# Decode attention on one core: five of eight block copies moved from VectorE to GpSimd, and 96 identity transposes between pairs on TensorE

## The chip, the core and the metric

The kernel runs on one core of a Trainium2 chip. The core has a matrix engine (TensorE, PE in the profile, with its weight loads as PEld), VectorE (DVE), ScalarE (ACT), GpSimd (POOL) and SyncE (SP), and 16 DMA engines that move data between HBM and the on-chip memory SBUF. Each engine works through its own queue in order; engines wait for each other by semaphores. TensorE writes to PSUM, and other engines take the results from there. The metric is the device time of one execution in microseconds (us).

## The reference

Attention for a single query position, with 32 query heads that share 8 key and value heads in groups of four, 65,536 keys and a head width of 128, all in bf16.

```python
B, Hq, Hkv, Sq, Sk, D = 1, 32, 8, 1, 65536, 128
k = jnp.repeat(k, rep, axis=1)          # rep = 4
v = jnp.repeat(v, rep, axis=1)
scores = jnp.einsum("bhqd,bhkd->bhqk", q, k) * D ** -0.5
p = jax.nn.softmax(scores, axis=-1)
return jnp.einsum("bhqk,bhkd->bhqd", p, v)
```

K and V have 134 MB each, and every byte is read once.

## The kernel before

**Tiles and stages.** The keys of one head are split into four units of 16,384 keys; a unit is 128 partitions by T = 128 columns of keys, 4 MB of K and 4 MB of V. Two units make a pair, and NP = 16 pairs are worked through one after the other: two pairs for each of the eight heads. In each pair the even unit is n = 0 and the odd unit n = 1.

**Buffers.** `kbuf` has room for two units of K, `vbuf` for two of V, and `bbuf` for one more unit of K. In the pairs 1 to 12 (`WHOLE = (1, 13)`) one DMA loads both units of K into `kbuf`, and engines then copy the odd unit into `bbuf` in eight blocks of 128 x 2048 elements (`CB = 16` columns each), so that `kbuf` is free for the next pair while the odd unit is still being worked on. In the pairs 0, 13, 14 and 15 the odd unit's K is loaded straight into `bbuf`, and no copies run.

**Order of loads.** SyncE issues all loads in a written-out order: K of a pair, then V of it, then K of the next. The K load of pair p waits for `kfree` (the even unit of the pair before is transposed) and for 2p counts of `cfree` (its copies are done; two engines count one each per pair). The V load waits for `vfree` (the pair before has used its V). Loads run one behind the other in the DMA queue, so that a load that is issued before the one ahead of it has landed follows it without a hole.

**Work of a pair on TensorE** (`pe_pair`). For each of 16 groups of eight columns a unit's K is transposed into PSUM (`pe_transposes`, L131; four buffers `trb`), and three groups later (`LAG = 3`) the scores are computed from the evicted transposes `ktb` (`pe_scores`, L140). The odd unit's groups follow the even unit's in the same stream. Then come the products with V of both units (`pe_values`, L157, with the rescaled sum of the unit before added at L150). Before the first group of a load TensorE waits for that load, and in the odd unit before each block of 16 columns for the copy of that block (`cpd` if VectorE made it, `cpa` if ScalarE).

**Evictions and copies.** VectorE evicts three of four groups from PSUM to `ktb` (L196), ScalarE each fourth (L193). Between evictions of the even unit VectorE copies the blocks 0, 1, 2 (after group 2) and 3, 4 (after group 8) at L203, and ScalarE the blocks 5, 6 and 7 (after groups 3, 7 and 11) at L342. `copy_unit` holds the condition on the lap: outside the pairs 1 to 12 it only counts the semaphores.

**Softmax.** VectorE reduces a unit's scores to a maximum for each partition (`chunk_max`, L228), GpSimd takes the maximum over partitions (L373), VectorE forms the new running maximum (`new_max`, L238 to L240), ScalarE the exponentials (L333). In VectorE's queue the `new_max` of the even unit stands between the odd unit's evictions 4 and 5. At the end of a head GpSimd adds the sums over partitions (L375). GpSimd has no other work in the loop.

**Loops.** TensorE's loop has a turn for each pair, those of VectorE, ScalarE and GpSimd one for each head, so two pairs.

Of the kernel before, what the change touches and what calls it, by code (L numbers as in the profile page):

```python
# [10 lines left out]
P = 128  # L11
T = 128
TB = 8
# [2 lines left out]
NKG = 8  # L16
LAG = 3
CB = 16
HU = 4
Q = 32  # L20

# [4 lines left out]


WHOLE = (1, 13)
DVE_COPIES = {2: (0, 1, 2), 8: (3, 4)}
ACT_COPIES = {3: (5,), 7: (6,), 11: (7,)}  # L30

OUT_ROWS = ((16, 12), (15, 13), (14, 9, 5), (11, 10, 6, 1))
# [2 lines left out]
def on_act(j):  # L35
    return j % 4 == 3


def starts(sizes):
    return [sum(sizes[:i]) for i in range(len(sizes))]  # L40


def take(e, sem, n=1):

    e.wait_ge(sem, n)
    e.sem_inc(sem, -n)  # L46


def bass_standalone__gqa_softmax__decode_kernel(nc, q, k, v, out):
    _, Hq, _, D = q.shape  # L50
    _, H, Sk, _ = k.shape
    R = Hq // H
    HR = H * R
    NU = H * HU
    NP = NU // 2
    assert HR == Q and all(sum(x) == HR - R for x in OUT_ROWS) and D == P and Sk == P * T * HU and T * R == 512 and H >= 3 and HU == 4
    scale = float(D) ** -0.5
# [5 lines left out]
    def sb(name, shape, dt):  # L63
        return S(nc.sbuf_tensor(name, shape, dt))

    def sem(name):
        return S(nc.semaphore(name))
# [10 lines left out]
    ident = sb("ident", [P, P], DT.bfloat16)  # L78
# [21 lines left out]
    trb = [S(nc.psum_tensor(f"trb{i}", [P, TB * P], DT.bfloat16)) for i in range(NTB)]  # L100
# [4 lines left out]
    kp = [[sem(f"kp{i}_{p}") for p in range(len(K_PIECES[i]))] for i in range(2)]  # L105
    vp = [[sem(f"vp{i}_{p}") for p in range(len(V_PIECES[i]))] for i in range(2)]
    kfree, cfree, bfree = sem("kfree"), sem("cfree"), sem("bfree")
    cpd, cpa = sem("cpd"), sem("cpa")
    vfree = sem("vfree")
    trd, tra, evd, eva = sem("trd"), sem("tra"), sem("evd"), sem("eva")  # L110
    qkd, qrdy, pvd = sem("qkd"), sem("qrdy"), sem("pvd")
# [2 lines left out]
    xd, xa, xg = sem("xd"), sem("xa"), sem("xg")  # L114
# [3 lines left out]
    def own(e, ins, s):  # L118
        ins.then_inc(s, 1)
        take(e, s)  # L120


    def pe_transposes(pe, n, j):
        kv = (bbuf if n else kbuf)[:, 0:T * D].rearrange("p (t d) -> p t d", d=D)
        if j * TB in starts(K_PIECES[n]):
            take(pe, kp[n][starts(K_PIECES[n]).index(j * TB)], 16)
        if n and j * TB % CB == 0:
            take(pe, cpa if j * TB // CB in sum(ACT_COPIES.values(), ()) else cpd)
        for i in range(TB):
            t = j * TB + i  # L130
            ins = pe.transpose(trb[j % NTB][:, i * P:(i + 1) * P], kv[:, t, :], ident[:, :])  # L131
        ins.then_inc(tra if on_act(j) else trd, 1)

    def pe_scores(pe, n, j):
        take(pe, eva if on_act(j) else evd)
        if n == 0 and j == 0:
            take(pe, qrdy)
        for i in range(TB):
            t, off = j * TB + i, (j % NKG * TB + i) * P
            ins = pe.matmul(qkb[n][:, t * R:(t + 1) * R], lhsT=ktb[:, off:off + P],  # L140
                            rhs=qcur[:, :], start=True, stop=True)
        if j == G - 1:
            ins.then_inc(qkd, 1)

    def pe_values(pe, n):
        vv = vbuf[:, n * T * D:(n + 1) * T * D].rearrange("p (t d) -> p t d", d=D)
        for t in range(T):
            if t == T - V_PIECES[1][-1]:
                take(pe, acr)
                pe.matmul(pvb[n][:, 0:R], lhsT=identf[:, :], rhs=acc[:, :], start=False, stop=False)  # L150
            if t == 0:
                take(pe, vp[n][0], 16)
                take(pe, exd)
            piece = vp[n][starts(V_PIECES[n]).index(t)] if t and t in starts(V_PIECES[n]) else None
            if piece:
                pe.wait_ge(piece, 16)
            ins = pe.matmul(pvb[n][:, 0:R], lhsT=vv[:, t, :], rhs=pts[n][:, t * R:(t + 1) * R],  # L157
                            start=t == 0, stop=t == T - 1)
            if piece:
                pe.sem_inc(piece, -16)  # L160
        ins.then_inc(pvd, 1)

    def pe_pair(pe):
        pend = []
        for n in range(2):
            for j in range(G):
                pe_transposes(pe, n, j)
                pend.append((n, j))
                if len(pend) > LAG:
                    pe_scores(pe, *pend.pop(0))  # L170
        while pend:
            pe_scores(pe, *pend.pop(0))
        for n in range(2):
            pe_values(pe, n)

    def tensor_engine(pe):
        pe.wait_ge(q_sem, 16)
        pe.wait_ge(t_id, 1)
        pe.transpose(qps[:, 0:HR], qsb[:, :], ident[0:HR, 0:HR]).then_inc(s_x, 1)
        pe.wait_ge(t_if, 1)  # L180
        with pe.Fori(0, NP):
            pe_pair(pe)
        pe.wait_ge(t_f, H)
        pe.transpose(trb[0][0:R, 0:P], oT[:, HR - R:HR], ident[:, :]).then_inc(s_x, 1)  # L184

# [12 lines left out]
    def copy_unit(e, lap, second, copies, op, done, x):  # L198

        def copies_now():  # L200
            for c in copies:
                off = T * D + c * CB * D
                ins = op(bbuf[:, c * CB * D:(c + 1) * CB * D], kbuf[:, off:off + CB * D])  # L203
                if c != copies[-1]:
                    ins.then_inc(done, 1)
            own(e, ins, x)
            e.sem_inc(done, 1)

        lo, hi = ((w - second + 1) // 2 for w in WHOLE)
        with e.If(lap < hi):  # L210
            if lo:
                with e.If(lap >= lo):
                    copies_now()
                with e.Else():
                    e.sem_inc(done, len(copies))
            else:
                copies_now()
        with e.Else():
            e.sem_inc(done, len(copies))
# [7 lines left out]
    def chunk_max(e, n):  # L227
        e.tensor_reduce(cmax[:, :], qkb[n][:, :].rearrange("p (t g) -> p g t", g=R),  # L228
                        AX.X, ALU.max).then_inc(cm, 1)
# [19 lines left out]
            own(e, e.tensor_tensor(lp[:, :], lp[:, :], alpha[:, :], ALU.mult), xd)  # L249
            own(e, e.tensor_tensor(lp[:, :], lp[:, :], rsum[:, :], ALU.add), xd)  # L250

    def dve_pair(e, second, lap):

        fresh, last = not second, second
        if fresh:
            e.memset(acc[:, :], 0.0).then_inc(acr, 1)
        for j in range(G):
            if not on_act(j):
                evict(e, 0, j)
            if j in DVE_COPIES:  # L260
                copy_unit(e, lap, second, DVE_COPIES[j], e.tensor_copy, cpd, xd)
                if j == max(DVE_COPIES):
                    e.sem_inc(cfree, 1)
        for j in (0, 1, 2):
            evict(e, 1, j)
        take(e, qkd)
        chunk_max(e, 0)
        evict(e, 1, 4)
        new_max(e, 0, fresh)
        for j in (5, 6, 8, 9, 10):  # L270
            evict(e, 1, j)
        rescale(e, 0, fresh)
        if fresh:
            own(e, e.tensor_copy(otmp[:, 0:HR - R], oT[:, R:HR]), xd)
            own(e, e.tensor_copy(oT[:, 0:HR - R], otmp[:, 0:HR - R]), xd)
            e.transpose(orow[:, :], oT[:, :]).then_inc(t_o, 1)
        for j in (12, 13, 14):
            evict(e, 1, j)
        take(e, qkd)
        chunk_max(e, 1)  # L280
        if last:
            next_queries(e)
        else:
            e.sem_inc(qrdy, 1)
        new_max(e, 1, False)
        take(e, pvd)
        rescale(e, 1, False)
        if last:
            e.sem_inc(lrd, 1)
            take(e, lra)  # L290
            own(e, e.reciprocal(recip[:, :], la[:, :]), xd)
        e.wait_ge(pvd, 1)
        if last:
            e.tensor_tensor(oT[:, HR - R:HR], pvb[1][:, 0:R], recip[:, :], ALU.mult).then_inc(t_f, 1)  # L294
        e.sem_inc(pvd, -1)
        e.sem_inc(vfree, 1)  # L296
# [16 lines left out]
    def vector_engine(e):  # L313
        make_identity(e)
        own(e, e.memset(oT[:, :], 0.0), xd)
        e.wait_ge(s_x, 1)
        own(e, e.tensor_copy(qT[:, :], qps[:, 0:HR]), xd)
        next_queries(e)
        with e.Fori(0, H) as lap:
            dve_pair(e, False, lap)  # L320
            dve_pair(e, True, lap)
        e.wait_ge(s_x, 2)
        e.tensor_copy(lrow[:, :], trb[0][0:R, 0:P]).then_inc(t_row, 1)  # L323

# [42 lines left out]
    def gpsimd_engine(e):  # L367
        own(e, e.memset(lw[:, :], 0.0), xg)
        own(e, e.partition_all_reduce(la[:, :], lw[:, :], P, bass.bass_isa.ReduceOp.add), xg)
        with e.Fori(0, H):  # L370
            for u in range(HU):
                take(e, cm)
                e.partition_all_reduce(cmaxa[:, :], cmax[:, :], P, bass.bass_isa.ReduceOp.max).then_inc(cma, 1)  # L373
            take(e, lrd)
            e.partition_all_reduce(la[:, :], lp[:, :], P, bass.bass_isa.ReduceOp.add).then_inc(lra, 1)  # L375
# [93 lines left out]
```

## Time and profile before

| | |
|---|---|
| median of 3 runs | 629.8 us (629.59 to 630.06) |
| the profiled execution, its own time | 631.18 us |
| its span, from the first to the last instruction | 629.8 us |
| HBM read | 268.44 MB, 426 GB/s over the span |
| busy: PE, PEld | 501.8 us (80%), 492.4 us (78%) |
| busy: DVE, ACT, POOL | 343.7 us (55%), 249.2 us (40%), 16.1 us (3%) |
| mean granted TensorE clock | 0.794 |

Busy time is that of the whole span. A row of a timeline gives the start, the duration, the engine, the line, the operation with output and input, the number of like instructions that it merges, and in brackets the idle time before it with what ended it. PEq, DVEq and so on are the sequencers of the engines, which handle waits and semaphores. A row of windows gives a stretch, its length, the busy time and instructions of PE, PEld, DVE, ACT and POOL, the granted TensorE clock (1.00 is full speed), the mean busy share of the DMA engines and what they moved in GB/s. The share is put together from whole packets and can come out over 1 in a short stretch. Ends of TensorE's matmuls are modelled, so rows of one stream overlap.

### The profile page before, as it was taken

Reading aid. Unit: us, or ns where it says so; the run is one execution under the profiler, and the core shown is the slowest. Engines: PE = TensorE matmul, PEld = TensorE weight load, DVE = VectorE, ACT = ScalarE, POOL = GpSimd, SP = SyncE. Lnnn points to the kernel's source line nnn. Section 1 sums busy time; section 2 is a strip of 40 time slices with the busy share of each in tenths; the row PEclk is TensorE's granted clock in tenths of the full one; section 3 lists DMA queues with packets and bytes.
Section 4 is the critical chain, followed back from the end, with each engine's and each line's share of the span. In section 5 each row is a group of like instructions: output and inputs, shape, how many; then the busy total and the mean of one; then the engine's idle time right before and its main releaser. Section 6 shows DMA issues by size and latency. Waiting matters only on the chain. (4 is left out here: it accounts for less than half of the span.)

```text
span 629.8 us, 28624 instructions
## 1 busy us (share of the span) xinstructions
PE 501.8 (80%) x12354; PEld 492.4 (78%) x12354; DVE 343.7 (55%) x735; ACT 249.2 (40%) x447; POOL 16.1 (3%) x46
## 2 busy tenths in 40 slices
PE   5753896969969599696996968879697799889896
PEld 5743886958968599686986968879697799889895
DVE  4530763818548185471845718467283665647381
ACT  2320642616436164361644517345172552514151
POOL 0000000000000000000000000000000000000000
PEclk9875885958869588795977959779597897869595
DMA  8999999999999999999999999999999999999997
GB/s 356 438 448 422 437 429 437 429 433 433 437 425 425 450 420 445 416 445 408 454 416 433 429 437 429 437 429 441 425 450 416 450 408 458 408 433 431 417 439 288
DMA packets 7635, 268.59 MB, mean 426 GB/s; under 512 B 1096, under 2 KB 1096, under 8 KB 1992
## 3 DMA queue, kind: packets, MB, share of 16 engines
q1 hardware_dynamic: 7576, 268.45, 99.2%
q8 instruction: 6, 0.10, 0.1%
q14 instruction: 5, 0.04, 0.0%
q10 hardware_dynamic: 48, 0.01, 0.0%
HBM read 268.44 MB, written 0.01 MB: 426 GB/s over the span
## 5 line engine op out<-in xcount | busy, mean ns | idle before, releaser
L196 DVE COPY ktb<-trb 128x1024 bf16<-128x1024 bf16 x384 | 249.7, 688 | 161.1 <-DVEq L46 156.8
L193 ACT ACTIVATE ktb<-trb 128x1024 bf16<-128x1024 bf16 x128 | 131.1, 1024 | 321.9 <-ACTq L46 321.9
L131 PE MATMUL trb<-ident,kbuf 128*128 128x128 bf16 x2048 | 177.1, 244 | 69.5 <-PEq L46 69.5
L131 PEld LDWEIGHTS trb<-ident,kbuf 128*128 128x128 bf16 x2048 | 143.9, 111 | 70.6 <-issue 70.6
L140 PE MATMUL qkb<-qcur,ktb 128*128 128x4 bf16 x4096 | 175.9, 165 | 25.0 <-PEq L46 24.2
L140 PEld LDWEIGHTS qkb<-qcur,ktb 128*128 128x128 bf16 x4096 | 155.9, 97 | 31.1 <-issue 30.2
L131 PE MATMUL trb<-ident,bbuf 128*128 128x128 bf16 x2048 | 156.8, 219 | 4.4 <-issue 4.4
L157 PEld LDWEIGHTS pvb<-pts,vbuf 128*128 128x128 bf16 x4096 | 119.3, 104 | 25.3 <-issue 24.1
L157 PE MATMUL pvb<-pts,vbuf 128*128 128x4 bf16 x4096 | 117.6, 166 | 23.6 <-PEq L46 13.3
L131 PEld LDWEIGHTS trb<-ident,bbuf 128*128 128x128 bf16 x2048 | 117.4, 97 | 4.6 <-issue 4.6
L342 ACT ACTIVATE bbuf<-kbuf 128x2048 bf16<-128x2048 bf16 x36 | 68.5, 1902 | 0.0
L333 ACT ACTIVATE pts<-qkb,negm 128x128 bf16<-128x128 f32 x128 | 50.8, 548 | 0.0
L203 DVE COPY bbuf<-kbuf 128x2048 bf16<-128x2048 bf16 x60 | 38.0, 684 | 0.0
L333 ACT ACTIVATION_READ_ACCUMULATOR pts<-qkb,negm 128x1 f32 x128 | 35.6, 278 | 0.0
L228 DVE TENSOR_REDUCE cmax<-qkb 128x4 f32<-128x512 f32 x32 | 21.9, 686 | 16.8 <-DVEq L46 16.8
L247 DVE TENSOR_TENSOR acc<-pvb,alpha 128x4 f32<-128x4 f32 x24 | 3.9, 162 | 46.0 <-DVEq L46 45.9
L373 POOL PARTITION_ALL_REDUCE cmaxa<-cmax x32 | 11.9, 371 | 567.9 <-POOLq L46 567.9
L329 ACT ACTIVATE alpha<-dm 128x4 f32<-128x4 f32 x24 | 4.9, 202 | 46.2 <-ACTq L46 46.2
L150 PE MATMUL pvb<-acc,identf 128*128 128x4 f32 x64 | 18.2, 354 | 0.0
L150 PEld LDWEIGHTS pvb<-acc,identf 128*128 128x128 f32 x64 | 16.1, 312 | 0.0
L294 DVE TENSOR_TENSOR oT<-pvb,recip 128x4 bf16<-128x4 f32 x8 | 1.3, 162 | 17.4 <-PE pvb L157 17.4
L238 DVE TENSOR_TENSOR m<-m,cmaxa 128x4 f32<-128x4 f32 x24 | 3.9, 163 | 8.0 <-DVEq L46 7.8
(38 smaller groups left out, 39.6 us busy)
## 6 DMA issues: line engine op xcount, KB each, us to landing
vbuf<-in_v_dram SPq DMA_DIRECT2D x5, 4096.0 KB, 30.2
bbuf<-in_k_dram SPq DMA_DIRECT2D x4, 2048.0 KB, 22.0
kbuf<-in_k_dram SPq DMA_DIRECT2D x2, 4096.0 KB, 19.3
bbuf<-in_k_dram SPq DMA_DIRECT2D x2, 4096.0 KB, 18.6
kbuf<-in_k_dram SPq DMA_DIRECT2D x2, 2048.0 KB, 18.9
kbuf<-in_k_dram SPq DMA_DIRECT2D x4, 512.0 KB, 12.1
kbuf<-in_k_dram SPq DMA_DIRECT2D x2, 1024.0 KB, 14.5
vbuf<-in_v_dram SPq DMA_DIRECT2D x1, 2048.0 KB, 30.2
```

The source lines that it names most:

```text
L131: ins = pe.transpose(trb[j % NTB][:, i * P:(i + 1) * P], kv[:, t, :], ident[:, :])
L140: ins = pe.matmul(qkb[n][:, t * R:(t + 1) * R], lhsT=ktb[:, off:off + P], rhs=qcur[:, :], start=True, stop=True)
L150: pe.matmul(pvb[n][:, 0:R], lhsT=identf[:, :], rhs=acc[:, :], start=False, stop=False)
L157: ins = pe.matmul(pvb[n][:, 0:R], lhsT=vv[:, t, :], rhs=pts[n][:, t * R:(t + 1) * R], start=t == 0, stop=t == T - 1)
L193: e.activation(dst, trb[j % NTB][:, :], AF.Copy).then_inc(eva, 1)
L196: e.tensor_copy(dst, trb[j % NTB][:, :]).then_inc(evd, 1)
L203: ins = op(bbuf[:, c * CB * D:(c + 1) * CB * D], kbuf[:, off:off + CB * D])
L228: e.tensor_reduce(cmax[:, :], qkb[n][:, :].rearrange("p (t g) -> p g t", g=R), AX.X, ALU.max).then_inc(cm, 1)
L329: e.activation(alpha[:, :], dm[:, :], AF.Exp, scale=scale)
L333: ins = e.activation(pv[:, g, :], sv[:, g, :], AF.Exp, bias=negm[:, g:g + 1], scale=scale, accum_out=rsum[:, g:g + 1])
L342: return e.activation(o, i, AF.Copy)
L373: e.partition_all_reduce(cmaxa[:, :], cmax[:, :], P, bass.bass_isa.ReduceOp.max).then_inc(cma, 1)
```

## The change

GpSimd copies blocks 0 to 4 of the odd unit, in one go, after VectorE has queued the eviction of the pair's first group (`pgo`); VectorE copies none any more. The semaphore `cpd` becomes `cpg`, and GpSimd gives the second count of `cfree`. The max over partitions stands behind the copies in GpSimd's queue. After the products with V of a pair, in the laps 0 to 11, TensorE transposes the identity matrix into the PSUM buffer `trb0`, six turns of a loop with 16 transposes each; nobody reads the result. In the laps 12 to 15 the condition skips it.

```diff
+WARM = 6
-DVE_COPIES = {2: (0, 1, 2), 8: (3, 4)}
+POOL_COPIES = (0, 1, 2, 3, 4)
 ACT_COPIES = {3: (5,), 7: (6,), 11: (7,)}
...
-    cpd, cpa = sem("cpd"), sem("cpa")
+    cpg, cpa, pgo = sem("cpg"), sem("cpa"), sem("pgo")
...
         if n and j * TB % CB == 0:
-            take(pe, cpa if j * TB // CB in sum(ACT_COPIES.values(), ()) else cpd)
+            take(pe, cpa if j * TB // CB in sum(ACT_COPIES.values(), ()) else cpg)
...
-    def pe_pair(pe):
+    def pe_pair(pe, lap):
...
         for n in range(2):
             pe_values(pe, n)
+        with pe.If(lap < WHOLE[1] - 1):
+            with pe.Fori(0, WARM):
+                for i in range(16):
+                    pe.transpose(trb[0][:, 0:P], ident[:, :], ident[:, :])
...
-        with pe.Fori(0, NP):
-            pe_pair(pe)
+        with pe.Fori(0, NP) as lap:
+            pe_pair(pe, lap)
...
-    def dve_pair(e, second, lap):
+    def dve_pair(e, second):
...
             if not on_act(j):
                 evict(e, 0, j)
-            if j in DVE_COPIES:
-                copy_unit(e, lap, second, DVE_COPIES[j], e.tensor_copy, cpd, xd)
-                if j == max(DVE_COPIES):
-                    e.sem_inc(cfree, 1)
+            if j == 0:
+                e.sem_inc(pgo, 1)
...
-        with e.Fori(0, H):
+        with e.Fori(0, H) as lap:
             for u in range(HU):
+                if u % 2 == 0:
+                    take(e, pgo)
+                    copy_unit(e, lap, u // 2, POOL_COPIES, e.tensor_copy, cpg, xg)
+                    e.sem_inc(cfree, 1)
                 take(e, cm)
                 e.partition_all_reduce(cmaxa[:, :], cmax[:, :], P, bass.bass_isa.ReduceOp.max).then_inc(cma, 1)
```

More of the change, by code (lines that the diff above doesn't have):

```diff
@@ L318, in vector_engine @@
         next_queries(e)
-        with e.Fori(0, H) as lap:
-            dve_pair(e, False, lap)
-            dve_pair(e, True, lap)
+        with e.Fori(0, H):
+            dve_pair(e, False)
+            dve_pair(e, True)
         e.wait_ge(s_x, 2)
```

## The prediction

> **What bounds the kernel now.** I read the DMA busy share by stretches first, then SyncE's issues, then TensorE's timeline around one pair, then VectorE and ScalarE in the same stretch.
>
> ```profile
> 99.00:500.00 401.00, 320.88 (x7890) 315.08 (x7891) 227.31 (x472) 173.86 (x289) 9.58 (x25) 0.79 1.00 432
> 500.00:590.00 90.00, 81.81 (x2112) 80.87 (x2109) 52.62 (x113) 34.00 (x75) 2.66 (x7) 0.82 0.99 427
> 590.00:626.00 36.00, 31.49 (x782) 31.05 (x779) 19.49 (x42) 11.47 (x26) 1.17 (x3) 0.78 0.99 418
> ...
> 593.04 33.03 DMA vbuf<-in_v_dram
> ```
>
> The last three columns are TensorE's granted clock, the DMA share and GB/s. The 16 DMA engines are full (share 1.00, 432 GB/s) for 401 us, and the chain that ended last is one load of V until 626.07. The time is the transfer of 268 MB, provided that the next transfer is always issued before the running one ends. So I ask of every edit only whether it makes an issue late.
>
> ```profile
> 193.33 0.33 SPq L399 DMA_DIRECT2D kbuf<-in_k_dram  x1
> 213.71 0.33 SPq L420 DMA_DIRECT2D vbuf<-in_v_dram  x1
> 233.01 0.33 SPq L399 DMA_DIRECT2D kbuf<-in_k_dram  x1
> 253.55 0.33 SPq L420 DMA_DIRECT2D vbuf<-in_v_dram  x1
> ```
>
> ```profile
> 219.51 3.57 PE L131 MATMUL trb<-ident,kbuf 128*128 128x128 bf16 x32 [6.11 <-PEq L46]
> 222.88 0.40 PE L140 MATMUL qkb<-qcur,ktb 128*128 128x4 bf16 x8
> ...
> 232.71 0.61 PE L131 MATMUL trb<-ident,bbuf 128*128 128x128 bf16 x8
> ...
> 244.67 3.17 PE L157 MATMUL pvb<-pts,vbuf 128*128 128x4 bf16 x120
> ...
> 252.87 0.35 PE L157 MATMUL pvb<-pts,vbuf 128*128 128x4 bf16 x8
> 258.12 3.41 PE L131 MATMUL trb<-ident,kbuf 128*128 128x128 bf16 x32 [4.90 <-PEq L46]
> ...
> 271.33 0.61 PE L131 MATMUL trb<-ident,bbuf 128*128 128x128 bf16 x8
> ...
> 296.84 3.57 PE L131 MATMUL trb<-ident,kbuf 128*128 128x128 bf16 x32 [5.34 <-PEq L46]
> ```
>
> TensorE starts a pair when its K has landed: 219.51, 258.12, 296.84, a period of (296.84-219.51)/2 = 38.7 us. It works until 253.22 (33.7 us) and 291.50 (33.4 us), so P = 33.55 us, and stands still about 5.2 us. The V load of the next pair is issued at 253.55, when the products with V are done, 4.6 us before the running K load lands. The K load is issued at 233.01, 13.5 us after the start, while V needs half a period, 19.35 us. These two margins are what the change can use up; nothing it gains beyond them shortens the transfer.
>
> **The change: the transposes of the identity.** A block of 96 follows pairs 0 to 11. Its price hangs on the clock.
>
> ```profile
> 209.50:212.50 3.00, 3.00 (x116) 3.00 (x116) 0.47 (x3) 0.00 (x0) 0.00 (x0) 0.50 1.06 459
> ...
> 258.10:261.10 3.00, 2.98 (x29) 3.00 (x30) 1.49 (x3) 0.00 (x0) 0.00 (x0) 0.50 1.06 459
> 261.60:264.60 3.00, 2.52 (x61) 2.35 (x57) 2.46 (x5) 2.82 (x2) 0.00 (x0) 1.00 0.81 350
> 297.00:302.00 5.00, 5.00 (x61) 5.00 (x60) 3.68 (x6) 1.47 (x2) 0.00 (x0) 0.50 1.03 446
> ```
>
> ```profile
> 195.81 0.61 PE L131 MATMUL trb<-ident,bbuf 128*128 128x128 bf16 x8
> 196.25 0.34 PE L140 MATMUL qkb<-qcur,ktb 128*128 128x4 bf16 x8
> ```
>
> The four-column products with V leave the clock at 0.50 though TensorE is busy all the time. The next pair starts cold and is granted 1.00 after 3.0 us (start 258.12) to 5.2 us (start 296.84). A cold transpose takes 3.37/32 = 0.105 us (219.51 to the first scores at 222.88), a warm one 0.44/8 = 0.055 us. So 28 to 49 of the 96 run cold and the other 68 to 47 warm: 6.7 to 7.7 us, middle 7.2.
>
> The block sits in a loop of six turns under a condition, which no row shows on TensorE.
>
> ```profile
> 523.39 0.35 PE L157 MATMUL pvb<-pts,vbuf 128*128 128x4 bf16 x8
> 523.61 3.57 PE L131 MATMUL trb<-ident,kbuf 128*128 128x128 bf16 x32
> ...
> L256 DVE MEMSET acc<- 128x4 f32 x8 | 0.5, 62 | 4.1 <-issue 3.7 <-DVEq L46 0.3
> ```
>
> At one turn of the outer loop TensorE goes on 0.22 us after its last eight products with V began, as within a row: the turn cost nothing, because instructions were queued ahead. VectorE lost 3.7/7 = 0.53 us at each of its turns. Bounds 0 and 6 x 0.53 = 3.2 us; I take 0.3, nearest TensorE's own rows. The block is W = 7.5 us (6.7 to 10.9) where the gap was 5.2.
>
> After pair 0 the gap is longer, but there code may still be on its way:
>
> ```profile
> 46.80 1.52 PE L157 MATMUL pvb<-pts,vbuf 128*128 128x4 bf16 x51 [6.10 <-issue]
> ...
> 63.66 3.37 PE L131 MATMUL trb<-ident,kbuf 128*128 128x128 bf16 x32 [7.11 <-PEq L46]
> ```
>
> 7.5 against 7.11 makes pair 1 late by x0 = 0.4 us; one more stall like the 6.10 (waiting on nothing the profile shows, in the first lap alone) would make it 6.5. I take 0.4.
>
> **What the even unit gains.** VectorE loses its copies, and TensorE starts warm.
>
> ```profile
> 220.67 0.69 DVE L196 COPY ktb<-trb 128x1024 bf16<-128x1024 bf16 x1 [10.31 <-DVEq L46]
> ...
> 222.99 1.89 DVE L203 COPY bbuf<-kbuf 128x2048 bf16<-128x2048 bf16 x3
> 225.41 2.49 DVE L196 COPY ktb<-trb 128x1024 bf16<-128x1024 bf16 x4 [0.54 <-DVEq L46]
> 227.82 1.28 DVE L203 COPY bbuf<-kbuf 128x2048 bf16<-128x2048 bf16 x2
> ```
>
> ```profile
> 223.21 1.02 ACT L193 ACTIVATE ktb<-trb 128x1024 bf16<-128x1024 bf16 x1 [14.05 <-ACTq L46]
> ...
> 226.44 1.02 ACT L193 ACTIVATE ktb<-trb 128x1024 bf16<-128x1024 bf16 x1 [0.42 <-ACTq L46]
> ...
> 233.06 1.02 ACT L193 ACTIVATE ktb<-trb 128x1024 bf16<-128x1024 bf16 x1 [0.55 <-ACTq L46]
> ```
>
> The even unit takes 13.2 us (219.51 to 232.71) whether the clock rises early (258.12 to 271.33) or late: two engines that copy between evictions set it. VectorE loses 1.89 + 1.28 = 3.2 us of copies, and is no limit after that. ScalarE keeps a cycle of 3.23 us (223.21 to 226.44) for four blocks, against TensorE's 4 x 0.645 = 2.6 (0.44 + 0.20 a block). Warm, the first four transposed blocks take 1.8 us in place of 3.4, so ScalarE's first eviction starts 2.1 us into the pair (now 3.7) and its fourth at 2.1 + 3 x 3.23 = 11.8, done at 12.8. TensorE reaches the odd unit at 1.78 + 12 x 0.645 + 0.2 = 9.7, plus some 0.7 for ScalarE's third eviction: 10.4. There it waits about 0.6 for the fourth. The rest, 244.67 - 232.71 = 11.96 us, is in step with TensorE and stays. The products with V begin 10.4 + 0.6 + 12.0 = 23.0 us after the start, now 25.2: 2.1 us gained, between 1.6 (ScalarE's earlier start alone) and 2.8 (no wait for ScalarE).
>
> Sum for a lap: W - gap - gain = 7.5 - 5.2 - 2.1 = +0.2 us (bounds -1.3 to +4.1). Each lap starts 0.2 us later against its K; after eleven such blocks 0.4 + 2.2 = 2.6 us. How late may it be?
>
> ```profile
> qsb<-in_q_dram ACTq DMA_DIRECT2D x1, 8.0 KB, 3.0
> ```
>
> A transfer of 8 KB takes 3.0 us from issue to landing, nearly all latency; a load issued that long ahead leaves no hole. Shortened, the pair takes 31.45 us, the V issue 0.3 more (252.87 + 0.35 to 253.55): cushion 38.7 - 31.45 - 0.3 - 3.0 = 4.0 us. 2.6 fits, so the DMA stays full.
>
> **GpSimd's copies** (12 pairs x 5). GpSimd has no such row. The same copy takes ScalarE 1.90 us and VectorE 1.89/3 = 0.63.
>
> ```profile
> L342 ACT ACTIVATE bbuf<-kbuf 128x2048 bf16<-128x2048 bf16 x36 | 68.5, 1902 | 0.0
> ...
> L368 POOL MEMSET lw<- 128x4 f32 x1 | 0.1, 103 | 0.3 <-POOLq L454 0.3
> ```
>
> ```profile
> 235.36 0.68 DVE L228 TENSOR_REDUCE cmax<-qkb 128x4 f32<-128x512 f32 x1
> ...
> 236.25 0.37 POOL L373 PARTITION_ALL_REDUCE cmaxa<-cmax  x1 [29.60 <-POOLq L46]
> ```
>
> Lower bound 0.63. Upper: VectorE's slowest row per element, 0.68/512, times 2048 is 2.7 us, times GpSimd against VectorE on the same memset, 103/62 = 1.66, is 4.5. I take c = 1.9, the row of the engine that does this very copy beside it. [...]
>
> GpSimd waits on `pgo` (after VectorE's first eviction) and ends near 1.6 + 5c = 11.1 us into the pair. Queued behind: the max over partitions, asked for 10.4 + 0.6 + 2.65 (232.71 to 235.36) + 0.9 = 14.5 us in. VectorE's `new_max` waits for it with the odd unit's evictions behind; TensorE waits for those. Before that, TensorE's `take(cpg)` holds each two blocks, the fifth at about 16 us; and SyncE's K issue waits for both `cfree`, ScalarE's near 12. All three are covered at 1.9. Cover ends at c = 2.6 (1.6 + 13 = 14.6). The DMA issues keep their order and number. On the tail, the untaken branch costs 0.1 us at most beside VectorE's last product.
>
> **Sum.** The profiled execution took 631.18 us, its span 629.8, 1.38 around it; plus 0.1 gives 631.3, or 629.9 on the scale of the three runs (median 629.8).
>
> **Rivals.**
>
> B, the TensorE loop becomes the bound. Same sum with a lap surplus above (4.0 - 0.4)/11 = 0.33 us; only 0.13 from mine. At +0.8 (longer cold stretch, costlier turns): 11 x 0.8 + 0.4 - 4.0 = 5.2 us of empty DMA, 635. For it: the closeness. Against: turns are hidden in the row at 523.61.
>
> C, GpSimd too slow, deciding from c = 2.6. At c = 3.2 it ends at 17.6, 3.1 late, about 1.0 of it VectorE's slack: surplus 0.2 + 2.1 = 2.3, cushion 1.9, 11 x 2.3 + 0.4 - 1.9 = 23.8: 654. At 4.5: 8.6 late, 11 x 8.8 + 0.4 + 4.6 = 102: 732.
>
> D, the identity does not warm: 96 x 0.105 + 0.3 = 10.4, gain only some 0.8 from the copies: surplus 10.4 - 5.2 - 0.8 = 4.4, cushion 2.6, 11 x 4.4 + 0.4 - 2.6 = 46: 676. Against it: 29 transposes and no score run from 258.10 to 261.10, and the clock is 1.00 right after. [...]
>
> E, faster: if the last 126 us ran at 432 GB/s, 90 x 5/432 + 36 x 14/432 = 2.2 us, 627.6. For it: 427 and 418. Against: the share there is already 0.99, so no late issue is there to mend.
>
> **How the numbers follow.** Forecast 0.46, B 0.32, C 0.13, D 0.02, E 0.07. A measurement of this kernel tells 0.2%, 1.26 us, from no change. Slower 0.32 + 0.13 + 0.02 = 0.47, same 0.46, faster 0.07. The forecast alone spans 629.2 to 631.1. The range reaches up through B into C to 645 (c near 3.0), leaving out the dear end of C and D, and down to 628.8, leaving most of E.
>
> **What would show it.** Windows of the DMA at 1.00 and 432 GB/s between 99 and 500; V issued at least 3 us before K lands. Identity transposes 6.7 to 7.7 us a block, clock 1.00 at a pair's start; the odd unit 10.4 us after it. GpSimd's copies 1.9 us by spacing. Wrong would be: starts of pairs over 38.8 us apart, or VectorE waiting in `new_max` for GpSimd.

## The result and the profile after

| | before | after |
|---|---|---|
| median of 12 runs | 629.89 us (629.48 to 632.34) | 633.06 us (631.36 to 635.61) |
| span of the profiled execution | 629.8 us | 632.3 us |
| busy: PE, DVE, POOL | 501.8, 343.7, 16.1 us | 572.5, 310.1, 126.8 us |

The ratio is 1.0045, with a 95% interval of 1.0034 to 1.0057: slower by about 3 us. The time lies inside the predicted range, but only because that range was drawn wide enough to take in rival B; the likeliest case of the prediction (no change, 629.9) is not what happened, its rival B (TensorE's lap becomes the bound, 635) is. A lap is the time from the start of one pair to the start of the next.

Windows of the middle, first the second stretch of the kernel before, then both stretches of the changed kernel; the last three columns are TensorE's granted clock, the DMA share and GB/s:

```profile
250.00:500.00 250.00, 199.45 (x4909) 195.91 (x4907) 140.00 (x292) 106.56 (x175) 6.18 (x16) 0.79 1.00 432
...
60.00:250.00 190.00, 178.85 (x4230) 175.35 (x4229) 95.87 (x205) 84.16 (x143) 50.80 (x38) 0.86 1.00 434
250.00:500.00 250.00, 237.19 (x5476) 233.00 (x5474) 118.44 (x254) 102.77 (x173) 64.32 (x48) 0.84 1.00 427
```

The first 190 us run at the full rate. The loss begins after 250 us: 427 in place of 432 GB/s over 250 us is 2.9 us. The share reads 1.00 in both stretches; only the GB/s show the holes, the times in which the next load has not yet begun to move data. So nothing is lost per pair from the start, as a price of the new work would be. Something runs out.

TensorE's timeline of the changed kernel, two laps:

```profile
213.48 7.33 PE L180 MATMUL trb<-ident 128*128 128x128 bf16 x96
220.64 1.95 PE L133 MATMUL trb<-ident,kbuf 128*128 128x128 bf16 x32
...
231.21 0.61 PE L133 MATMUL trb<-ident,bbuf 128*128 128x128 bf16 x8
...
233.74 0.34 PE L142 MATMUL qkb<-qcur,ktb 128*128 128x4 bf16 x8 [0.63 <-PEq L48]
...
244.01 3.31 PE L159 MATMUL pvb<-pts,vbuf 128*128 128x4 bf16 x120
...
252.47 8.27 PE L180 MATMUL trb<-ident 128*128 128x128 bf16 x96
260.57 1.95 PE L133 MATMUL trb<-ident,kbuf 128*128 128x128 bf16 x32
...
291.96 7.34 PE L180 MATMUL trb<-ident 128*128 128x128 bf16 x96
```

TensorE no longer stands still between pairs: the first transposes of a pair follow the block of identity transposes at once, with no idle time in brackets. Two laps from block to block take 291.96 - 213.48 = 78.48, so 39.24 us each; the eleven laps from the first block (56.40) to the last (487.95) take 39.23. K comes every 38.7 us as long as no load is late (the landings at 218.27 and 256.98). Each lap is therefore late by another 0.53 us.

SyncE's issues of V in the changed kernel:

```profile
213.93 0.33 SPq L428 DMA_DIRECT2D vbuf<-in_v_dram  x1
...
252.94 0.33 SPq L428 DMA_DIRECT2D vbuf<-in_v_dram  x1
...
292.41 0.33 SPq L428 DMA_DIRECT2D vbuf<-in_v_dram  x1
```

By the landings in the trace the K load in flight ends at 218.27, 256.98 and 296.29. V is issued 4.34, 4.04 and 3.88 us ahead of it, and lands 38.70, 39.30 and 39.56 us after the V before. The hole opens between the first and the second of these. The lead, the time by which V is issued ahead of the landing of K, shrinks on the way there: 6.02, 5.36 and 5.09 us in the three pairs before (V issued at 96.14, 135.51 and 174.48), all without a hole. From the issue at 252.94 on, seven V loads, with leads of 3.88 to 4.42 us, land 0.17 to 0.85 us late; together that is 3.5 us.

The prices of the parts, from the page, the windows and ScalarE's timeline of the changed kernel:

```profile
L209 POOL COPY bbuf<-kbuf 128x2048 bf16<-128x2048 bf16 x60 | 110.8, 1893 | 166.4 <-POOLq L48 166.4
```

```profile
213.50:217.25 3.75, 3.75 (x41) 3.75 (x39) 0.00 (x0) 0.00 (x0) 0.00 (x0) 0.50 0.97 419
217.35:220.60 3.25, 3.25 (x62) 3.25 (x60) 0.00 (x0) 0.00 (x0) 0.00 (x0) 1.00 1.04 446
252.60:258.20 5.60, 5.60 (x56) 5.60 (x54) 0.23 (x2) 0.00 (x0) 0.00 (x0) 0.50 1.01 410
```

```profile
222.72 1.02 ACT L199 ACTIVATE ktb<-trb 128x1024 bf16<-128x1024 bf16 x1 [13.33 <-ACTq L48]
...
232.57 1.02 ACT L199 ACTIVATE ktb<-trb 128x1024 bf16<-128x1024 bf16 x1 [0.55 <-ACTq L48]
```

GpSimd's copy takes 1.89 us (1.9 was assumed, from ScalarE's row). The granted clock goes from 0.50 to 1.00 3.8 and 5.8 us after the block's start (213.48 to 217.30, 252.47 to 258.26), and the pair starts at 1.00. ScalarE's fourth eviction starts 232.57 - 220.64 = 11.9 us into the pair (11.8 was worked out), and TensorE waits for it at 233.74. The odd unit is 0.84 us longer than before, 12.80 us (231.21 to 244.01) in place of 11.96, and that wait is most of it.

### The profile page after: what moved, and what is told of

The parts are those of the page before. It is cut to its first block, busy times and chain, and to the rows that moved or that the text cites. A ratio compares the mean times of both kernels' runs of the same rounds, so it can differ in the third digit from the quotient of the medians.

```text
span 632.3 us, 31084 instructions
## 1 busy us (share of the span) xinstructions
PE 572.5 (91%) x13506; PEld 562.0 (89%) x13506; DVE 310.1 (49%) x675; ACT 249.2 (39%) x447; POOL 126.8 (20%) x106
## 5 line engine op out<-in xcount | busy, mean ns | idle before, releaser
L133 PE MATMUL trb<-ident,kbuf 128*128 128x128 bf16 x2048 | 155.4, 225 | 4.6 <-PEq L48 4.6
L209 POOL COPY bbuf<-kbuf 128x2048 bf16<-128x2048 bf16 x60 | 110.8, 1893 | 166.4 <-POOLq L48 166.4
L133 PEld LDWEIGHTS trb<-ident,kbuf 128*128 128x128 bf16 x2048 | 123.7, 101 | 4.9 <-issue 4.9
L180 PE MATMUL trb<-ident 128*128 128x128 bf16 x1152 | 93.5, 263 | 0.0
L180 PEld LDWEIGHTS trb<-ident 128*128 128x128 bf16 x1152 | 91.7, 123 | 0.0
L381 POOL PARTITION_ALL_REDUCE cmaxa<-cmax x32 | 11.9, 370 | 294.2 <-POOLq L48 294.2
L152 PEld LDWEIGHTS pvb<-acc,identf 128*128 128x128 f32 x64 | 16.1, 312 | 0.0
## 6 DMA issues: line engine op xcount, KB each, us to landing
kbuf<-in_k_dram SPq DMA_DIRECT2D x4, 512.0 KB, 11.8
```

Source lines behind the costliest of these rows:

```text
L180: pe.transpose(trb[0][:, 0:P], ident[:, :], ident[:, :])
```

## The experiments

Two theories were set against each other. T: TensorE's lap, 39.23 us, is longer than the DMA's 38.7, and the lateness uses up the time by which V is issued ahead. G: GpSimd's copies disturb the loads or hold K's issue.

**The copies alone.** The changed kernel without the block of identity transposes:

```diff
-        with pe.If(lap < WHOLE[1] - 1):
-            with pe.Fori(0, WARM):
-                for i in range(16):
-                    pe.transpose(trb[0][:, 0:P], ident[:, :], ident[:, :])
```

> The changed kernel without the identity transposes; GpSimd still copies five blocks. Theory T (TensorE's lap is longer than the DMA's, 39.23 us against 38.7): without the block the lap is about 31.75 plus some 1.3 for the cold start, 33 us, TensorE stands still again for over 5 us, V is issued over 5 us ahead of the landing of K, and the time is that of before, 629.9 within 0.7. Theory G (GpSimd's copies disturb the loads, or hold K's issue): it stays at 632 to 634.

Measured: 630.39 us, ratio 1.0001 (0.9991 to 1.0010). G falls: 60 copies on GpSimd cost nothing that shows within 0.1%. V is issued 4.6 to 5.3 us ahead from 97.77 on, where over 5 was expected. TensorE's timeline of this kernel:

```profile
218.58 3.57 PE L133 MATMUL trb<-ident,kbuf 128*128 128x128 bf16 x32 [5.71 <-PEq L48]
...
230.86 0.61 PE L133 MATMUL trb<-ident,bbuf 128*128 128x128 bf16 x8
...
243.66 3.30 PE L159 MATMUL pvb<-pts,vbuf 128*128 128x4 bf16 x120
...
257.30 3.57 PE L133 MATMUL trb<-ident,kbuf 128*128 128x128 bf16 x32 [5.04 <-PEq L48]
```

The even unit is shorter, 12.28 us in place of 13.20, but the products with V begin 25.08 us into the pair in place of 25.16: what VectorE gave is lost again in the odd unit, which takes 12.80 in place of 11.96. Over the pairs 1 to 12 the products begin 24.73 to 25.08 us in, 24.93 in the mean.

**The block alone.** The kernel before with the same lines added, VectorE copying:

> The kernel before with the identity transposes alone; VectorE copies. Theory T: the lap loses the gain of the moved copies, so it is 7.65 for the block and 32.5 to 33.2 for the pair, 40.2 to 40.9 us against 38.7: with a cushion of some 1.5 us, 11 x 1.5 to 2.2 less 1.5 is 15 to 23 us lost, 645 to 653. Theory G: 629.9, as GpSimd does nothing new.

Measured: 643.8 us, ratio 1.0216 (1.0198 to 1.0234). The way is T's, the size at the lower edge: 13.6 us lost where 15 to 23 were expected. TensorE's timeline of this kernel:

```profile
216.91 6.78 PE L180 MATMUL trb<-ident 128*128 128x128 bf16 x96
223.53 1.95 PE L133 MATMUL trb<-ident,kbuf 128*128 128x128 bf16 x32
...
235.81 0.61 PE L133 MATMUL trb<-ident,bbuf 128*128 128x128 bf16 x8
...
247.84 3.20 PE L159 MATMUL pvb<-pts,vbuf 128*128 128x4 bf16 x120
...
256.21 7.58 PE L180 MATMUL trb<-ident 128*128 128x128 bf16 x96
...
295.96 8.15 PE L180 MATMUL trb<-ident 128*128 128x128 bf16 x96
```

The products with V begin 24.31 us into the pair: the warm start alone gains 0.85 us, the copies alone 0.1 to 0.4 (0.25 in the mean), both together (244.01 - 220.64 = 23.37) 1.8. The block's length varies from lap to lap, and the two laps shown, 39.30 and 39.75 from block to block, are among the shorter ones. The ten laps from the start of pair 2 (104.08) to that of pair 12 (505.16) take 40.11 in the mean, just under the 40.2 that was the least expected. With a pair of 32.65 us (32.5 to 32.8) and the lead of about 4 us found below, the cushion is 38.7 - 32.65 - 0.3 - 4.0 = 1.75 us, and 11 x 1.41 - 1.75 = 13.8.

**The length of the block.** The last 16 transposes of a block run warm, 0.056 us apart in the changed kernel (the first 16 are 0.104 apart), so their price is known; only `WARM` changes.

```diff
-WARM = 6
+WARM = 5      # and 8 in the other kernel
```

> The changed kernel with 80 identity transposes in place of 96. The last 16 are warm, 16 x 0.055 = 0.89 us. Theory T: lap 39.23 - 0.89 = 38.3 us, under the DMA's 38.7; no hole, 629.9 within 0.7. Theory G: unchanged, 632 to 634. If a fixed price per block (its condition, its start) were the cause, the time would fall by less than a third of the loss.

> The changed kernel with 128 identity transposes. Two turns more are 32 x 0.055 = 1.78 us a lap. Theory T: every us of it is lost in full, 11 x 1.78 = 19.6 over the changed kernel's 633, so 650 to 655. Theory G: 632 to 635.

Measured: with 80 transposes 629.46 us, ratio 0.9990 (0.9981 to 1.0000); with 128 transposes 651.93 us, ratio 1.0349 (1.0335 to 1.0364). Sixteen transposes fewer, 0.89 us a lap, take away the whole loss: by the sum the lap of 39.23 becomes 38.34, under 38.7, so TensorE has to wait for K again. TensorE's timeline of the kernel with 80 shows such a wait:

```profile
289.17 6.80 PE L180 MATMUL trb<-ident 128*128 128x128 bf16 x80
296.23 1.95 PE L133 MATMUL trb<-ident,kbuf 128*128 128x128 bf16 x32 [0.26 <-PEq L48]
```

Thirty-two more cost 651.93 - 633.06 = 18.9 us, where 11 x 1.78 = 19.6 was expected. A knee on one side and the full slope on the other: that is a second engine taking over the bound, not a price for each block.

**A shorter pair with the whole block.** ScalarE gives one of its three copies to GpSimd:

```diff
-POOL_COPIES = (0, 1, 2, 3, 4)
-ACT_COPIES = {3: (5,), 7: (6,), 11: (7,)}
+POOL_COPIES = (0, 1, 2, 3, 4, 5)
+ACT_COPIES = {3: (6,), 7: (7,)}
```

> The changed kernel with all 96 identity transposes, but GpSimd copies six blocks and ScalarE two. If ScalarE's three copies set the pair's length once TensorE is warm, as the sum had it: its cycle drops out for one of three turns, the pair falls from 31.75 to some 30.7 to 31.0 us, the lap from 39.23 to 38.2 to 38.5, under the DMA's 38.7: 629.9. GpSimd ends near 1.2 + 6 x 1.85 = 12.3 us, still ahead of the 13.5 at which the maximum is asked for. If ScalarE is not the limit: 633.

Measured: 629.84 us, ratio 1.0000 (0.9991 to 1.0009), with all 96 transposes in place. TensorE's timeline of this kernel:

```profile
249.57 8.13 PE L180 MATMUL trb<-ident 128*128 128x128 bf16 x96
...
268.21 0.61 PE L133 MATMUL trb<-ident,bbuf 128*128 128x128 bf16 x8
...
280.23 3.22 PE L159 MATMUL pvb<-pts,vbuf 128*128 128x4 bf16 x120
...
288.25 7.59 PE L180 MATMUL trb<-ident 128*128 128x128 bf16 x96
```

The odd unit takes 280.23 - 268.21 = 12.02 us, without the wait of the changed kernel (12.80), and the lap 38.68, the DMA's pace. The pair itself falls from 31.75 us to 31.1, with the even unit no shorter (10.67 us for 10.57). So it was the wait for ScalarE's cycle of eviction and copy at the start of the odd unit that took a warm pair over the DMA's pace, and half a us less a lap is all it takes. The run also answers a rival that T and G leave out, that 96 transposes disturb the loads by themselves: they are all there, and nothing is lost.

**How far ahead a load must be issued.** The copies on GpSimd, no block between pairs, but 32 or 48 warm transposes inside the pair, ahead of the products with V. Against the kernel with the copies alone:

```diff
         while pend:
             pe_scores(pe, *pend.pop(0))
+        with pe.If(lap < WHOLE[1] - 1):
+            with pe.Fori(0, WARM):        # 2 and 3
+                for i in range(16):
+                    pe.transpose(trb[0][:, 0:P], ident[:, :], ident[:, :])
         for n in range(2):
             pe_values(pe, n)
```

> GpSimd's copies, no block between the pairs, but 32 warm identity transposes (1.78 us) inside each of the pairs 0 to 11, ahead of the products with V, of which some 0.6 us lie in a wait that was there. TensorE's lap stays under 38.7 us, so only the V issue moves, from 4.6 to 5.0 us ahead of the landing of K to 3.4 to 3.8. If 3.0 us are enough for the next load to follow without a hole (the prediction's cushion): 629.9. If 4.4 are needed (the loads of the changed kernel that met an empty queue landed 23.7 us after their issue, 19.35 of it transfer): half of the missing 0.6 to 1.0 a lap, 11 x 0.3 to 0.5, 633 to 636.

> The same with 48 transposes (2.67 us, 2.1 of it felt): V is issued 2.5 to 2.9 us ahead. With 3.0 us needed: 630.5 to 633. With 4.4 needed: 11 x 0.75 to 0.95, 638 to 641.

Measured: with 32 transposes 631.6 us (630.66 to 635.52), ratio 1.0039 (1.0022 to 1.0056); with 48 transposes 637.38 us, ratio 1.0120 (1.0103 to 1.0137). The first is between the two cases and decides little: in its profile, which is that of its fastest run, V is still issued 4.1 to 4.5 us ahead, for more of the inserted work than expected lay in waits that were there. The second is the clear one. SyncE's issues of V and TensorE's starts of pairs in it:

```profile
179.91 0.33 SPq L428 DMA_DIRECT2D vbuf<-in_v_dram  x1
216.76 0.33 SPq L428 DMA_DIRECT2D vbuf<-in_v_dram  x1
256.82 0.33 SPq L428 DMA_DIRECT2D vbuf<-in_v_dram  x1
295.58 0.33 SPq L428 DMA_DIRECT2D vbuf<-in_v_dram  x1
```

```profile
181.36 3.57 PE L133 MATMUL trb<-ident,kbuf 128*128 128x128 bf16 x32 [1.77 <-PEq L48]
221.45 3.57 PE L133 MATMUL trb<-ident,kbuf 128*128 128x128 bf16 x32 [5.00 <-PEq L48]
260.15 3.45 PE L133 MATMUL trb<-ident,kbuf 128*128 128x128 bf16 x32 [3.66 <-PEq L48]
299.59 3.57 PE L133 MATMUL trb<-ident,kbuf 128*128 128x128 bf16 x32 [4.33 <-PEq L48]
338.29 3.57 PE L133 MATMUL trb<-ident,kbuf 128*128 128x128 bf16 x32 [1.78 <-PEq L48]
```

TensorE waits here for K at each start, so a start marks a landing. V issued 4.7 and 4.0 us ahead of it (216.76, 295.58): the next K is there 38.70 us later, no hole. Issued 3.3 us ahead (256.82): 39.44, a hole of 0.7. Issued 1.5 us ahead (179.91): 40.09, a hole of 1.4. The need in this run is about 4 us, not 3.0, and it is no sharp threshold. The row issued 1.5 us ahead would give a need of 2.8; the V loads issued at 98.86 and 492.42, 3.3 and 3.4 us ahead of the landing, are late by 1.5 and 2.0, which would give 4.8 and 5.4; and the changed kernel has late loads at leads up to 4.42 and one on time at 4.34.

The landings tell more. The trace has 16 counts for the end of each load, and between 90 and 495 us the first comes 1.5 to 2.6 us before the last in the kernel before and in the changed kernel (254.92 and 256.98 for one K load of the latter). In the ten profiles of this study 208 loads are issued between 90 and 495 us. Counted from the first report of the load ahead, 32 of 35 issued less than 2.0 us before it are late (they land over 0.1 us later than 19.35 us after the load ahead), 8 of 23 at 2.0 to 2.5 us, and 6 of 150 above that; in the changed kernel alone it is 3 of 3, 4 of 8 and none of 10. Counted from the last report the edge is less clear: 22 of 43 are late at 3.0 to 4.5 us. So in these traces the time ahead of the first report, with an edge at some 2.5 us, tells late loads from the others better than the time ahead of the last does; no run was made to test it.

**The last pair's pieces.** On the kernel with 80 transposes, the even K of the last pair in two loads in place of four:

```diff
-                    if p in (0, NP - 1):
+                    if p == NP - 1 and n == 0:
+                        e.dma_start(to[:, 0:W // 2], s[:, 0:W // 2]).then_inc(kp[0][0], 16)
+                        tokens(kp[0][1:3])
+                        e.dma_start(to[:, W // 2:W], s[:, W // 2:W]).then_inc(kp[0][3], 16)
+                    elif p in (0, NP - 1):
                         pieces(to, s, K_PIECES[n], kp[n])
```

> 80 identity transposes, and the last pair's even K in two halves in place of pieces of 16, 16, 32 and 64 columns. In the kernel before, that pair's K takes 20.4 us on the queue where others take 19.4. If small pieces are the cause, some 0.5 us come off: 629.0. If not, or if the later start of the pair is felt at the end: 629.5 to 630.5.

Measured: 629.4 us, ratio 0.9996 (0.9987 to 1.0005). The halves bring no gain that shows. The same pieces take 19.7 to 20.5 us in other profiled executions: 19.8 in the kernel with the copies alone (586.35 to 606.16 in the landings), 20.5 in the kernel with 80 transposes (586.64 to 607.11). So the 20.4 of the kernel before is no fixed price of the pieces; with the halves it is 19.6 in the one execution profiled. No kernel of this study is faster than the one before by more than its interval allows.

## Why the prediction went as it did

- *The DMA bounds the kernel, and an edit counts only by making an issue late.* Right. The copies alone, 80 transposes, and six copies on GpSimd all come out at the time of before, with TensorE busy for very different times.
- *GpSimd's copy, c = 1.9 us, no cost up to 2.6.* Right in size, by luck: the 1.9 was ScalarE's row, and nothing tied GpSimd's rate to it; the measured copy takes 1.89. It has no effect on the time, and rival C did not occur: in the pair that starts at 220.64 the copies end at 230.91, and GpSimd then stands idle for 4.2 us until the maximum is asked for at 235.12, 14.5 us into the pair as worked out.
- *The identity transposes warm the clock.* Right in the two blocks read: the clock is granted 1.00 after 3.8 and 5.8 us of identity transposes alone (windows 213.50 to 217.25 and 252.60 to 258.20 still at 0.50), and rival D fell.
- *The untaken branch costs 0.1 us at most.* An estimate that no row of before gave; right. In the changed kernel TensorE goes on 0.24 us after its last eight products with V began (527.25 to 527.49), where the kernel before took 0.22, and on the tail 0.63 us (629.94 to 630.57) in place of 0.60 (627.49 to 628.09).
- *x0 = 0.4 after the first pair.* Nearly right: the first block begins at 56.40, pair 1 at 63.59, 0.2 us after its K landed at 63.37. No second stall lay in between: the transposes follow the block with no idle time in brackets.
- *Sum for a lap: +0.2 us.* This step failed, by size: 39.23 - 38.7 = 0.53. The term that was mis-sized is the gain, 1.8 us in place of 2.1 (its own figures, 25.2 - 23.0, give 2.2): the even unit takes 10.57 us for 10.4, and the wait for ScalarE's fourth eviction costs 12.80 - 11.96 = 0.8 for 0.6. The block was right: counted as in the sum, from the end of a pair's last products to the next pair's start, it takes 7.0 and 8.0 us by turns, 7.5 in the mean of the pairs 2 to 11. With P = 33.55 the gap is 5.15, and 7.5 - 5.15 - 1.8 = 0.55. An error of 0.3 us is small beside the terms, but the surplus is a difference of terms that nearly cancel, and the point of decision was at 0.33. The sign that the prediction named for being wrong came: starts of pairs lie 39.23 us apart in the mean (39.9 and 38.6 by turns).
- *Cushion 4.0 us.* Mis-sized as well. The time needed ahead was taken from a transfer of 8 KB, 3.0 us; counted from the landing of the load ahead, as the prediction counts, the loads of this kernel need about 4. V was issued at least 3.88 us ahead in all of the pairs 1 to 12, so the sign that the prediction named for being right (3 us) was met, and loads were late all the same. Nor does a load follow without a hole whenever it is issued before the one ahead of it has landed, as the description of the loads has it: the one issued 3.3 us ahead left a hole of 0.7. With the pair 31.75 us long (220.64 to 252.61, and 260.57 to 292.10) the cushion is 38.7 - 31.75 - 0.3 - 4.0 = 2.65.
- The same formula with the measured terms: 11 x 0.53 + 0.2 - 2.65 = 3.4 us. The medians differ by 3.2, and the holes of the profiled execution add up to 3.5. So close a match is in part luck, since the 4 us are no sharp figure; 4.5 would give 3.9. Rival B named the mechanism and the formula; with a chance of 0.32 against 0.46 it stood second because the gain and the lead both erred in the direction that favoured no change. Rival E was argued down because the DMA share was 0.99; the changed kernel's share of 1.00 with holes shows that the share can't tell.

## What to carry to other kernels

Work put into an idle gap is free only as far as the gap is wider than the work less what it gives back; compare the lap of that engine with the lap of the bound, for here a surplus of 0.53 us in a lap of 39.23 was felt as soon as the slack that was saved up was gone. A loss that begins in the middle of the span can be slack running out, so look for it by windows, and in GB/s (here 427 against 432) rather than in the busy share (1.00 in both). Take the lead that a load needs from loads of the same size on a full queue (here about 4 us), not from a small one (3.0 us for 8 KB), and count it from the first report of the load ahead too, not only from its landing.

## What the runs showed of the hardware

The changes of the granted clock in the records lie whole steps apart: the 35 changes between 0.50 and 1.00 in the profile of the kernel before, and the 33 in that of the changed kernel, are all whole multiples of 3.413 us apart within their profile, whatever TensorE did in between. In the changed kernel the clock rises at 217.30, 258.26, 295.81 and 336.77: 12, 11 and 12 steps. With it goes the block's length there, 7.3 us in one lap and 8.3 in the next.

Single loads landed late, though issued well ahead, for no reason that the profile shows: in the profiled execution of the kernel before, starts of pairs lie 39.50 us apart once (180.01 to 219.51) where the neighbours have 38.7, with the loads of that lap issued over 4 us ahead. Three profiled executions have no load over 0.15 us late between 90 and 495 us; their spans are 628.0, 628.0 and 628.3 us (six copies on GpSimd, 80 transposes with the halves, and the copies alone), where the kernel before has 629.8. Where the delays come from stays open.
